# One woven stream against two passes: attention and token mixing of all pairs first, channel mixing afterwards

## The chip, the cores and the metric

One core of one Trainium2 chip. The metric is the device time of one execution in microseconds (us), the median of several executions. Everything is computed in fp32. On TensorE one fp32 matmul instruction leaves two records in the trace, and "records" below means those.

## The reference, cut to what matters

```python
# q, k, v: (8 batches, 8 heads, 576 tokens, 64 channels)
kv  = np.einsum('bhsd,bhse->bhde', k, v)
out = np.einsum('bhsd,bhde->bhse', q, kv)
rms = np.sqrt(np.mean(out * out, axis=-1, keepdims=True) + 1e-06)
x   = out / rms * g_norm                 # then to (batch, token, 512)

xt = x.transpose(0, 2, 1)                # token mixing, 576 -> 256 -> 576
u  = x + (np.maximum(xt @ w_tok1, 0.0) @ w_tok2).transpose(0, 2, 1)
h2 = np.maximum(u @ w_ch1, 0.0) @ w_ch2  # channel mixing, 512 -> 1536 -> 512
return u + h2
```

The four mixing weights arrive as float64. The kernel rounds them to fp32 on the chip with seven elementwise steps per piece ("decode"), each weight once. A batch has 576 = 4 x 128 + 64 tokens. Two batches make a pair, whose two leftovers of 64 tokens share one tile, so a pair has nine tiles and there are four pairs.

## The kernel before

Attention and token mixing of a pair ("the front") are woven, step by step, into the channel mixing of the pair before. The first front has nothing to be woven into. The decode of the token weights and of the first 12 pieces of channel weights is woven into it, and that of the other 12 into the first layer of channel mixing.

```python
def decode(dst, raw):                    # cut: names of operands kept
    nc.gpsimd.tensor_scalar(out=dst, in0=hi, ...)                 # 1 GpSimd
    nc.vector.tensor_scalar(out=dst, in0=dst, ... min, max)       # 2 VectorE
    nc.vector.tensor_scalar(out=bits, in0=bits, ... shift)        # 3 VectorE
    nc.vector.scalar_tensor_tensor(out=bits, in0=hi, in1=bits)    # 4 VectorE
    nc.vector.tensor_scalar(out=part, in0=bits, ... mask)         # 5 VectorE
    nc.vector.scalar_tensor_tensor(out=part, in0=lo, in1=part)    # 6 VectorE
    nc.gpsimd.tensor_tensor(out=dst, in0=dst, in1=part, op=ALU.add)  # 7 GpSimd

def kv(side, half):                      # k^T v, two heads' pairs at once
    for i in range(2):
        for j in range(JJ):              # the fifth piece has 64 rows only
            r = slice(0, P if j < J else HF)
            nc.tensor.matmul(ps[:, i], lhsT=k_in[r, j, ts(i, P)],
                             rhs=v_in[r, j, ts(i, P)], ...)

def norm(o_ps, i):                       # one tile of 128 tokens
    nc.scalar.activation(x3, o, AF.Square)
    nc.vector.tensor_reduce(ms, x3, ...)
    ...                                  # root and a Newton step, small
    nc.vector.tensor_mul(x3, o, inv.to_broadcast([P, H, D]))
    nc.gpsimd.tensor_mul(x3, x3, g_sb.to_broadcast([P, H, D]))

weave(steps, weights)                    # first front with 17 pieces of weights
for pair in range(B // 2):
    body = main(pair, X, U)              # channel mixing
    if pair == 0:
        weave(body[:NF], [do(get_ch2, f) for f in range(NF)])
        body = body[NF:]
    if pair + 1 < B // 2:
        X, U, fill = front(pair + 1)
    weave(body, fill)
```

## Time and profile before

| | before |
|---|---|
| time, median of 4 runs | 1053.81 us |
| span of the profiled execution | 1052.2 us |
| TensorE busy | 1002.1 us, 95% |
| VectorE, ScalarE, GpSimd busy | 25%, 10%, 10% |
| first token layer of the first pair | 60.4 to 80.9 us |
| channel weights decoded until | about 168 us |
| dense period of a pair | 244.96 us |

One view is added here: the chain of work that ended last, where channel mixing waits for the last piece of its weights. The columns are start, duration, engine, tile and line.

```profile
162.63 1.49 DVE w_ch L114
...
164.60 0.70 DVE w_ch L118
...
166.63 1.27 POOL w_ch L124
167.90 0.04 issue
167.94 2.08 PE ps_w L287 x2
```

The seven steps of a decode run one after the other on two engines, and TensorE starts the second layer of channel mixing (ps_w) 0.04 us after the last of them.

### The profile page before, as it was taken

What the parts mean: (1) busy time and instruction counts of PE and PEld (TensorE: products, weight loads), DVE (VectorE), ACT (ScalarE), POOL (GpSimd) and SP (SyncE); (2) the same over time, 40 slices, a digit from 0 to 9 for tenths busy, and PEclk for the clock granted to TensorE, in tenths of its full rate; (3) what the DMA queues carried; (4) which work ended last, traced back from release to release, by engine and by line L of the source; (5) the groups of instructions that cost most, each with busy time, mean ns of one, the idle gap of its engine ahead of it and who ended that gap; (6) DMA issues with size and microseconds to landing.
All of it is one profiled execution on the core that took longest, in us unless ns stands there. A gap on an engine that the chain in (4) does not pass through costs nothing.

```text
span 1052.2 us, 7658 instructions
## 1 busy us (share of the span) xinstructions
PE 1002.1 (95%) x3120; PEld 537.9 (51%) x3120; DVE 266.5 (25%) x559; ACT 100.8 (10%) x214; POOL 106.1 (10%) x100
## 2 busy tenths in 40 slices
PE   4788977999999999999999999999999999999998
PEld 3643544664455466554445456554445445454553
DVE  2898773351011113330111112240011111010000
ACT  0211100020001011111001011011001000000000
POOL 1464441120000001110000000010000000000000
PEclk9789997999999999999999999999999999999999
DMA  8943342121000031300000021000000000000000
GB/s 239 323 147 116 108 142 95 66 90 55 10 11 1 20 100 46 111 10 1 10 21 1 10 65 45 11 20 1 0 21 11 10 21 0 21 10 11 21 0 30
DMA packets 33554, 53.34 MB, mean 51 GB/s; under 512 B 2416, under 2 KB 20848, under 8 KB 33520
## 3 DMA queue, kind: packets, MB, share of 16 engines
q1 hardware_dynamic: 28928, 37.76, 11.0%
q10 hardware_dynamic: 4592, 15.11, 4.6%
q8 instruction: 24, 0.39, 0.2%
q14 instruction: 10, 0.08, 0.0%
HBM read 43.42 MB, written 9.44 MB: 50 GB/s over the span
## 4 chain that ended last, share of the span: by engine, by line
PE 84%; DVE 9%; DMA 4%; POOL 2%; issue 1%; ACTq 0%; ACT 0%; POOLq 0%
PE ps_w L287 35%; PE ps_v L273 33%; PE ps_h L224 4%; PE ps_u L235 4%; PE ps_kv L171 3%; PE ps_o L206 2%; DMA raw<-in_moe_w_tok_dram 2%; DVE part L122 2%; DVE w_ch L118 1%; DVE w_ch L116 1%; DVE w_ch L114 1%; PE ps_h L227 1%; PE ps_ut L250 1%; DVE part L120 1%; POOL w_ch L124 1%; DMA raw<-in_moe_w_ch_dram 1%
## 5 line engine op out<-in xcount | busy, mean ns | idle before, releaser
L287 PE MATMUL ps_w<-w_ch,v 128*128 128x512 f32 x864 | 385.0, 598 | 10.5 <-POOL w_ch L124 10.5
L273 PE MATMUL ps_v<-uT,w_ch 128*128 128x384 f32 x1152 | 383.8, 488 | 1.1 <-DVE v L279 1.1
L273 PEld LDWEIGHTS ps_v<-uT,w_ch 128*128 128x128 f32 x1152 | 215.0, 190 | 151.7 <-issue 13.4
L287 PEld LDWEIGHTS ps_w<-w_ch,v 128*128 128x128 f32 x864 | 161.7, 191 | 208.8 <-issue 190.9
L279 DVE TENSOR_SCALAR v<-ps_v 128x384 f32<-128x384 f32 x72 | 40.0, 556 | 266.2 <-PE ps_v L273 266.2
L201 POOL TENSOR_TENSOR x<-x,g_sb 128x512 f32<-128x512 f32 x36 | 47.8, 1328 | 519.5 <-DVE x L200 517.7
L291 DVE TENSOR_TENSOR o<-ps_w,x 128x512 f32<-128x512 f32 x36 | 24.9, 692 | 259.0 <-PE ps_w L287 258.9
L171 PE MATMUL ps_kv<-v_in,k_in 128*128 128x128 f32 (+1 forms) x320 | 56.0, 323 | 14.9 <-DMA v_in<-in_v_dram 13.8
L277 ACT ACTIVATE v<-ps_v 128x384 f32<-128x384 f32 x72 | 35.3, 490 | 355.2 <-PE ps_v L273 326.4
L235 PE MATMUL ps_u<-h,w_tok 128*128 128x512 f32 x128 | 60.3, 596 | 3.4 <-DVE x L243 3.3
L171 PEld LDWEIGHTS ps_kv<-v_in,k_in 128*128 128x128 f32 (+1 forms) x320 | 48.6, 219 | 27.1 <-issue 20.8
L224 PE MATMUL ps_h<-x,w_tok 128*128 128x512 f32 x128 | 59.7, 610 | 1.7 <-DVE ms L188 1.7
L243 DVE TENSOR_TENSOR x<-ps_u,x 128x512 f32<-128x512 f32 x36 | 24.8, 689 | 96.1 <-PE ps_u L235 78.3
L206 PEld LDWEIGHTS ps_o<-kvp,qT 128*128 128x128 f32 x256 | 37.1, 214 | 16.6 <-issue 4.4
L206 PE MATMUL ps_o<-kvp,qT 128*128 128x128 f32 x256 | 38.6, 302 | 7.1 <-DVE x L200 3.7
L251 ACT COPY uT<-ps_ut 128x512 f32<-128x512 f32 x36 | 21.0, 585 | 219.3 <-PE ps_ut L250 199.8
L187 DVE TENSOR_REDUCE ms<-x 128x8 f32<-128x512 f32 x36 | 24.5, 683 | 67.5 <-ACT x L185 67.5
L224 PEld LDWEIGHTS ps_h<-x,w_tok 128*128 128x128 f32 x128 | 24.7, 195 | 32.1 <-issue 28.9
L235 PEld LDWEIGHTS ps_u<-h,w_tok 128*128 128x128 f32 x128 | 23.8, 190 | 29.8 <-issue 21.1
L124 POOL TENSOR_TENSOR w_ch<-w_ch,part 128x512 f32<-128x512 f32 x24 | 31.4, 1308 | 36.7 <-DVE part L122 34.8
L185 ACT ACTIVATE x<-ps_o 128x512 f32<-128x512 f32 x36 | 21.5, 597 | 90.1 <-PE ps_o L206 75.3
L250 PEld LDWEIGHTS ps_ut<-ident,x 128*128 128x128 f32 x144 | 17.7, 141 | 20.8 <-issue 16.9
(38 smaller groups left out, 281.1 us busy)
## 6 DMA issues: line engine op xcount, KB each, us to landing
raw<-in_moe_w_ch_dram ACTq DMA_DIRECT2D x24, 512.0 KB, 3.6
qT<-in_q_dram SPq DMA_DIRECT2D x8, 1152.0 KB, 5.6
k_in<-in_k_dram SPq DMA_DIRECT2D x16, 512.0 KB, 3.7
v_in<-in_v_dram SPq DMA_DIRECT2D x16, 512.0 KB, 5.5
out_dram<-o SPq DMA_DIRECT2D x32, 256.0 KB, 2.0
raw<-in_moe_w_tok_dram ACTq DMA_DIRECT2D x2, 576.0 KB, 6.1
raw<-in_moe_w_tok_dram ACTq DMA_DIRECT2D x2, 512.0 KB, 9.2
k_in<-in_k_dram SPq DMA_DIRECT2D x16, 64.0 KB, 3.6
```

The costliest lines, as they stand in the source:

```text
L124: nc.gpsimd.tensor_tensor(out=dst, in0=dst, in1=part, op=ALU.add)
L171: nc.tensor.matmul(ps[:, i], lhsT=k_in[r, j, ts(i, P)], rhs=v_in[r, j, ts(i, P)], start=(j == 0), stop=(j == JJ - 1))
L201: nc.gpsimd.tensor_mul(x3, x3, g_sb.to_broadcast([P, H, D]))
L206: nc.tensor.matmul(ps[:, ts(hp, P)], lhsT=qT[side][:, hp, ts(j, P)], rhs=kvp[side][:, hp], start=True, stop=True)
L224: nc.tensor.matmul(ps, lhsT=w_tok1[:, j, ts(t, P)], rhs=X[side * J + j], start=(j == 0), stop=False)
L235: nc.tensor.matmul(ps, lhsT=w_tok2[:, t, ts(i % J, P)], rhs=h1[i // J][:, t], start=(t == 0), stop=(t == NTOK - 1))
L250: nc.tensor.transpose(ps[:, c], X[i][:, ts(c, P)], ident)
L273: nc.tensor.matmul(ps, lhsT=w_ch1[:, c, ts(f, P)], rhs=U[blk][:, c], start=(c == 0), stop=(c == NC - 1))
L277: nc.scalar.activation(dst, ps, AF.Relu)
L279: nc.vector.tensor_scalar(out=dst, in0=ps, scalar1=0.0, scalar2=None, op0=ALU.max)
L287: nc.tensor.matmul(ps, lhsT=v1[i // TB, part][:, f, ts(i % TB, P)], rhs=w_ch2[:, ft], start=(ft == 0), stop=(ft == NF - 1))
L291: nc.vector.tensor_tensor(out=o, in0=ps, in1=X[i], op=ALU.add)
```

## The change

The intent is to have TensorE never wait for channel weights, and to use larger and simpler matmuls. There are two passes. The first does attention and token mixing of all four pairs and stores the result u in DRAM; the channel weights are fetched and decoded behind it. The second reads u back in nine groups of 512 tokens and does channel mixing alone. k and v get zero rows so that each matmul of k-v has 128 rows; normalisation takes two tiles at a time; the 64-row matmuls of the two batches in the first token layer stand next to each other; the first decode step goes to ScalarE and the second to GpSimd.

```diff
@@ decode
-        nc.gpsimd.tensor_scalar(out=dst, in0=hi.bitcast(F32), scalar1=2.0 ** -112, scalar2=1.0,
-                                op0=ALU.mult, op1=ALU.mult)
-        nc.vector.tensor_scalar(out=dst, in0=dst, scalar1=TOP, scalar2=-TOP,
+        nc.scalar.activation(dst, hi.bitcast(F32), AF.Copy, scale=2.0 ** -112)
+        nc.gpsimd.tensor_scalar(out=dst, in0=dst, scalar1=TOP, scalar2=-TOP,
                                 op0=ALU.min, op1=ALU.max)
@@ kv
-                    r = slice(0, P if j < J else HF)
-                    nc.tensor.matmul(ps[:, i], lhsT=k_in[r, j, ts(i, P)],
-                                     rhs=v_in[r, j, ts(i, P)],
+                    nc.tensor.matmul(ps[:, i], lhsT=kk[:, j, ts(i, P)], rhs=vv[:, j, ts(i, P)],
@@ norm: two tiles (n = 2)
-            nc.gpsimd.tensor_mul(x3, x3, g_sb.to_broadcast([P, H, D]))
+            nc.gpsimd.tensor_mul(x3, x3, g_sb.to_broadcast([P, n * H, D]))
@@ first token layer, both sides of a pair
+            for side in range(2):
+                r = ds(side * HF, HF)
+                nc.tensor.matmul(ps[side], lhsT=w_tok1[r, J, ts(t, P)], rhs=x_of(pair, 8)[r], ...)
@@ the order of the whole (cut)
-    weights += [do(get_ch1, i, c) for i in range(DCH // 512) for c in range(NC)]
-    weave(steps, weights)
-    for pair in range(B // 2):
-        ...
+    weave(attention(0), weights)                # token weights only
+    weights = [do(get_ch1, i, c) for i in range(2) for c in range(NC)]
+    weights += [do(get_ch2, f) for f in range(NF)]
+    steps = []
+    for pair in range(B // 2 - 1):
+        weave([do(steps.append, f) for f in token_mixing(pair)],
+              [do(steps.append, f) for f in attention(pair + 1)])
+    weave(steps, weights)
+    ...
+    weave(token_mixing(3), prepare(0, ...))     # prepare: transposes of a group
+    ...
+    for g in range(NG):
+        fetch_u(g + 1)
+        for f in range(NF):
+            channel1(g, f)
+        weave(channel2(g), prepare(g + 1, t_psum))
```

## The prediction

> **What bounds the kernel now.** I read the busy strips first, then one table of stretches, then the end of the chain of waits, then the timeline of single steps. The strips are in 40 slices of 26.3 us, in tenths:
>
> ```profile
> span 1052.2 us, 7658 instructions
> ...
> PE   4788977999999999999999999999999999999998
> ...
> DVE  2898773351011113330111112240011111010000
> ...
> PEclk9789997999999999999999999999999999999999
> ```
>
> TensorE is short of work only in the first seven slices, exactly where VectorE is at 7 to 9, and there its clock is below full in several slices. The stretches give it in numbers (columns: us, then busy us of PE, PEld, DVE, ACT, POOL, then clock, DMA share, GB/s):
>
> ```profile
> 33.36:166.63 133.27, 107.35 (x350) 59.05 (x348) 109.67 (x206) 18.49 (x40) 63.50 (x60) 0.88 0.49 155
> ...
> 372.22:617.18 244.96, 244.96 (x782) 131.21 (x781) 43.91 (x104) 24.61 (x53) 11.40 (x9) 1.00 0.10 34
> 617.18:862.13 244.95, 244.95 (x781) 131.20 (x781) 43.89 (x104) 24.61 (x53) 11.40 (x9) 1.00 0.06 20
> 862.13:1052.20 190.07, 185.58 (x504) 95.41 (x503) 16.55 (x28) 9.41 (x19) 0.00 (x0) 1.00 0.04 14
> ```
>
> The middle two are the two undisturbed periods of a pair of batches: TensorE never idle, VectorE at 18%. The first runs from the first to the last decode of a channel weight: VectorE is 82% busy. The end of the chain of waits gives the parts of a period (start, us, what):
>
> ```profile
> 862.13 30.96 PE ps_v L273 x96
> 893.09 30.90 PE ps_w L287 x72
> ...
> 1016.81 30.91 PE ps_w L287 x72
> ...
> 1047.75 0.69 DVE o L291
> ```
>
> A block of channel mixing is 61.86 us, three are 185.58, so attention and token mixing of a pair ("the front") cost 244.96 - 185.58 = 59.38. Four dense pairs would be 979.8. The tail is 1052.2 - 1047.75 = 4.5. So 1052.2 - 979.8 - 4.5 = 67.9 us are lost at the start. Where in the start? Token mixing of the first pair begins at 60.4 in the timeline. By then only attention is done. From the same steps seen dense later, the front's 59.38 holds 18.4 us of first token layer (4 x (3.53 + 1.06)), 15.6 of second (8 x 1.72 + 1.87) and 4 of transposes (9 x 0.44), with which attention and the joints between steps come to about 20.6. So 40 us are lost by 60.4, and the other 28 later, when channel mixing waits for its weights.
>
> Single steps, dense:
>
> ```profile
> 377.22 2.97 PE L171 MATMUL ps_kv<-v_in,k_in 128*128 128x128 f32 x20
> ...
> 380.13 2.20 PE L273 MATMUL ps_v<-uT,w_ch 128*128 128x384 f32 x6
> ...
> 393.56 1.05 PE L206 MATMUL ps_o<-kvp,qT 128*128 128x128 f32 x8
> ...
> 394.45 1.78 PE L273 MATMUL ps_v<-uT,w_ch 128*128 128x384 f32 x5
> ...
> 471.23 1.12 PE L227 MATMUL ps_h<-x,w_tok 64*128 64x512 f32 x2
> ...
> 472.29 2.85 PE L273 MATMUL ps_v<-uT,w_ch 128*128 128x384 f32 x8
> ```
>
> Start to start (an fp32 matmul is two records): 20 records of k-v take 2.91 us, though 8 of the same width in attention take 0.89, or 0.111 each. Four of the twenty have only 64 rows. Two 64-row records of token mixing take 1.06, against 30.90/72 = 0.429 each for full ones of that width, 0.86.
>
> **What the Trainium skill says.** "TensorEngine Tiling (Array Packing)", Key Properties: a change of tiling mode drains TensorE. The trace agrees: 16 full records at 0.111 leave 2.91 - 1.78 = 1.13 us for four 64-row ones, 0.28 each. "TensorE: Matmul & The Clock Gate", The mechanism (Part 3): matmuls on different row groups run concurrently. This kernel never has two such neighbours; its two column halves in the left-over tile of the second token layer do overlap (8 records in 103.97 to 105.84, 1.87 us instead of 3.43). "SBUF — State Buffer", Who interferes with whom: GpSimd excludes a VectorE instruction with two SBUF inputs, or in a 2-port mode, for a whole instruction. It agrees:
>
> ```profile
> 95.34 0.41 DVE L116 TENSOR_SCALAR w_ch<-w_ch 128x512 uint32<-128x512 uint32 x1
> ...
> 98.58 1.38 POOL L124 TENSOR_TENSOR w_ch<-w_ch,part 128x512 f32<-128x512 f32 x1 [1.56 <-DVE part L122]
> 98.86 1.37 DVE L116 TENSOR_SCALAR w_ch<-w_ch 128x512 uint32<-128x512 uint32 x1
> ```
>
> The same shift takes 0.41 us alone and 1.37 beside GpSimd's add.
>
> **The change part by part.**
> TensorE work. Zero rows make every k-v matmul 128 rows: 20 x 0.111 = 2.22 instead of 2.91, 0.69 saved x 16 steps = 11 us. The two sides' 64-row matmuls of the first token layer become neighbours: twice 1.06 per pair of sides; if the second record of one side overlaps the first of the other, 3 x 0.43 + 0.2 = 1.5, saving 0.6 x 8 = 5; I take 6 for both this and fewer mode changes. Channel mixing has the same columns: 384 cost 30.96/96 = 0.3225 and 512 cost 0.429, so a column is as dear, and 288 records fewer save (0.3225 x 4/3 - 0.429) x 864 = 0.7 us. Total 979.8 - 17.7 = 962.
>
> Second pass. Tokens are transposed from a single buffer, four per group, the last one right before the first layer of the next group. Transposes to dependent matmul: 526.82 to the copy's start at 527.45 is 0.63, the copy 0.58, and say 0.07 to the matmul: 1.28, against 0.44 when other work follows (371.62 to 372.06). So 0.84 x 8 groups = 7 us of bubbles that before does not have. The tail stays 4.5. One hand-over between passes and one exposed ReLU in the last token mixing: 1 us.
>
> DRAM round trip. 9.44 MB written and read again. Reads are 1 MB, asked for one group (82 us) ahead; hidden. In the first pass 28.3 MB of q, k, v, 15.1 of weights and 9.4 stored, 53 MB in some 230 us, is 230 GB/s, against 323 in the second slice at a share of 0.98. Hidden on the mean.
>
> Start. Only the five token-weight pieces are woven into the first attention; the 24 channel-weight pieces (now 20, some larger) come after it. Before, the last k-v of the pair started at 38.17, set by transfers that mostly remain, but attention then took until 58.8 because VectorE was decoding channel weights (TensorE waited 3.7 us on the normalisation). Now: k-v until 41, three attention steps of 4 to 5 us until 46, a normalisation of two tiles about 8 until 54, overlapped with first-layer work and next-pair k-v of about 6. Attention now costs 20.6 - 2.8 = 17.8, so 54 - 17.8 - 6 = 30; I take 29 lost, instead of 40. The later 28 us of weight waits vanish as such.
>
> First pass, steady. Three stretches of token mixing plus the next attention: (59.38 - 4 - 4.3) x 3 = 153 us of TensorE. VectorE in it, by undisturbed durations: decode now has 4 instead of 5 operations here (0.43 + 0.69 + 0.43 + 0.69 = 2.24) x 24 = 54; normalisation of two tiles 1.22 + 1.22 + 0.8 (an estimate: 512 elements take 0.69, of which 0.53 is 512 elements at the 0.96 GHz that "Trainium Kernel Development and Optimization", NeuronCore Architecture, gives for VectorE; twice 0.53 and once the other 0.16; 0.8 for the five small steps of 0.11 to 0.2) 3.24 x 4 + 2.2 per pair, x 3 = 45; adds 27 x 0.69 = 19; copies 12 x 0.28 = 3. Sum 121. In the first stretch above the mean of a decode shift is 739 ns where its median is 428, of the step before it 604 against 426, of the mask 524 against 427: with the small steps that wait up to 1.36 us beside GpSimd, about 18 us of the 110 are such waiting, a fifth on top of the rest. With a fifth, 121 is 145. VectorE reached 82% there, held up by the chain GpSimd, VectorE, GpSimd of each piece and its two staging buffers. The weights are now thinner on the ground (20 pieces in 153 us, 7.7 us each, where that chain took 9.1 us for two), so I choose 86%: 145 / 0.86 = 168. So VectorE, not TensorE, bounds this stage by a little: 15 us more.
>
> Sum: 962 + 29 + 15 + 7 + 4.5 + 1 = 1018.
>
> **Rivals.** One: VectorE work hides completely. For it: the weights have 153 us instead of 133, VectorE gives up one operation per piece and half of its tiny normalisation steps. Against it: 145 of 153. Then 1003. Two: a new wait takes the old one's place. The first decode step moves from GpSimd to ScalarE, which also issues the weight transfers, so ScalarE can stand waiting for a transfer (3.6 us median to landing) with squares, ReLUs and k-v copies behind it. For it: before, ScalarE's uT copy already waited 12.4 us behind weight staging. Against: ScalarE is nearly idle, and TensorE has four-deep PSUM. At 2 us exposed for each of 20 pieces, 1055. Three: GpSimd, whose work on two tiles doubles the lock to about 2.5 us, stretches VectorE further: 10 to 20 more, 1030 to 1038. Four: transfers, if bursts of q, k, v, weights and stores collide: 10 more.
>
> **Range and chances.** The floor is rival one with a start better by 5: 998. Above, rival three plus some of two: 1040. Faster by 2% needs less than 1032.6 of 1053.7, which leaves 15 us for errors; I give that 0.78, within 2% 0.19, slower 0.03 (rival two at its full size).
>
> **What would show it.** Second pass: nine groups of 82.4 us, about 0.8 us idle before each first matmul, full clock, VectorE under 15%. k-v steps near 2.2 us. Token mixing starting near 46 to 54. First-pass stretch of 160 to 175 us from there to the last pair's token mixing, VectorE above 80%, TensorE short of work there. The prediction is wrong if TensorE is at 95% or more there (rival one), if ScalarE's longest waits are on the raw weight transfers (rival two), or if the second pass shows bubbles of several us.

## The result, and the profile after

The changed kernel takes 1054.62 us (median of 4 runs, 1053.17 to 1056.12) against 1053.81. The ratio is 1.0015, with a 95% interval of 0.9997 to 1.0033: the same time. A ratio here is the mean time of one kernel's fast runs over that of the other's in the same rounds, so it is not quite the ratio of the medians quoted. The predicted 1018 was missed by 37 us.

The page of the changed kernel, in the same 40 slices:

```profile
span 1052.0 us, 6896 instructions
...
PE   3759787899999999999999999999999999999998
...
DVE  2886877635210010001001001000000100100000
...
PEclk9879988999999999999999999999999999999999
```

The hole in TensorE's strip is as wide as before, seven to eight slices, and VectorE is again busy in just those. From slice 9 on little is left to gain. Next the three stretches of the first pass, each from the end of one pair's first token layer to that of the next (columns as in the prediction: the stretch, its length, busy us of PE, PEld, DVE, ACT, POOL, clock, DMA share, GB/s):

```profile
83.45:149.70 66.25, 55.67 (x242) 32.17 (x240) 52.29 (x85) 15.90 (x28) 31.53 (x24) 0.92 0.65 218
149.70:215.75 66.05, 56.30 (x243) 32.87 (x241) 41.87 (x72) 12.35 (x23) 21.74 (x16) 0.92 0.56 179
215.75:268.50 52.75, 51.10 (x242) 30.04 (x240) 23.27 (x48) 9.08 (x18) 10.67 (x5) 1.00 0.44 150
83.45:268.50 185.05, 163.07 (x722) 95.08 (x720) 117.44 (x204) 37.33 (x69) 63.94 (x45) 0.94 0.56 184
```

All three hold the same matmuls. The third, after the last decode, takes 52.75 us; the first two take 13.3 us more each. In neither is any engine full: over all three VectorE is at 117 of 185 us, or 63%, and TensorE at 88%. The granted clock is 0.92 in the first two, and the same 242 records keep TensorE busy some 5 us longer there than in the third; the other 8 to 9 us are idle.

What TensorE waits for in the first pass (waiter, releaser, us in total, times, longest):

```profile
PE ps_h L247 <- POOL x L212: 20.4, 8, 7.9
PE ps_o L219 <- ACT kvp L188: 13.8, 4, 6.2
PE ps_kv L184 <- DMA v_in<-in_v_dram: 13.1, 2, 12.8
PE ps_o L228 <- ACT kvp L188: 7.1, 2, 5.2
```

Before, 10.5 us of waits stood against the decode's last add (GpSimd, w_ch). That releaser is gone; in its place the first token layer (ps_h) waits 20.4 us for the last step of the normalisation, and attention (ps_o) 20.9 us for the copies of k-v on ScalarE. Both are steps that share engines with the decode.

The longest of these waits, step by step, in the order of the timeline (start, duration, engine, line, operation, tiles; an idle time in brackets):

```profile
55.28 1.41 DVE L130 SCALAR_TENSOR_TENSOR w_ch<-raw,w_ch 128x768 uint32<-128x768 uint32 x1
...
58.58 0.55 DVE L132 TENSOR_SCALAR part<-w_ch 128x768 uint32<-128x768 uint32 x1
...
60.35 3.08 POOL L212 TENSOR_TENSOR x<-x,g_sb 128x1024 f32<-128x1024 f32 x1 [4.46 <-DVE x L211]
61.16 2.31 DVE L206 SCALAR_TENSOR_TENSOR ms<-ms,inv 128x16 f32<-128x16 f32 x1
...
63.40 2.60 POOL L136 TENSOR_TENSOR w_ch<-w_ch,part 128x768 f32<-128x768 f32 x1
...
63.49 1.22 PE L247 MATMUL ps_h<-x,w_tok 128*128 128x512 f32 x1 [7.86 <-POOL x L212]
```

TensorE waits for the double tile that GpSimd multiplies at 60.35; it has stood idle for 7.86 us when that ends. Steps of channel-weight decode (here lines 130 and 132, 1.41 and 0.55 us) run on VectorE between the small steps of this tile's normalisation. While the multiply runs, a VectorE step on 16 elements per partition, which belongs to another tile, takes 2.31 us and ends when the multiply does. Two decodes of channel weights are in progress beside it (line 136 is the last step of one), although in the program the channel weights come after this attention. Their first transfer is issued at 32.3 us and their first decode step runs at 37.4 us: the order in the program text isn't the order on the engines.

The second pass, from the chain that ended last:

```profile
371.41 0.02 issue
371.43 0.59 ACT uT L293
372.02 0.04 issue
372.07 41.47 PE ps_v L311 x96
413.53 20.60 PE ps_w L325 x48
```

TensorE stands still from 371.41 to 372.07, 0.66 us between two groups, while ScalarE copies the last transposed tile. It does so eight times, 5.3 us in all by this chain; the run below that moves the transposes won back 760.4 - 755.9 = 4.5 us of it. The last matmul ends at 1047.35 us, as good as before (1047.75). The pass starts at 286.97 us, so it takes 760.4 us.

The steps of attention, dense (the numbers after the operation count records):

```profile
207.43 1.12 PE L251 MATMUL ps_h<-x,w_tok 64*128 64x512 f32 x2
...
214.69 1.13 PE L251 MATMUL ps_h<-x,w_tok 64*128 64x512 f32 x4
215.75 2.50 PE L184 MATMUL ps_kv<-v_in,k_in 128*128 128x128 f32 x20
218.08 1.88 PE L260 MATMUL ps_u<-h,w_tok 128*128 128x512 f32 x4
219.80 2.39 PE L184 MATMUL ps_kv<-v_in,k_in 128*128 128x128 f32 x20
222.03 1.88 PE L260 MATMUL ps_u<-h,w_tok 128*128 128x512 f32 x4
```

From start to start a k-v step takes 222.03 - 219.80 = 2.23 us, against 2.91 before. The 64-row matmuls are neighbours only in the second half of the layer, where four records take 215.75 - 214.69 = 1.06 us, the time of two. In the first half they stay apart.

In a table, with the prediction's parts. Its text gives 4.5 us for the tail and, for the second pass, nine groups of 82.4, eight times 1.76 of transposes and eight bubbles of 0.84, together 762. So its first pass ended at 1018 - 4.5 - 762 = 251.5; less 18.4 after the last first layer (15.6 of second layer, 1.8 of transposes, 1 of hand-over) and the 168 of the three stretches, its start is 65.

| us | predicted | after | run without channel weights |
|---|---|---|---|
| end of the first pair's first token layer | 65 | 83.5 | 72.0 |
| three stretches | 168 | 185.1 | 158.3 |
| from there to the second pass | 18.4 | 18.5 | 18.4 |
| start of the second pass | 251.5 | 287.0 | 248.75 |
| second pass to its last matmul | 762 | 760.4 | 760.4 |

The last column is an experiment told below. The whole miss lies ahead of the second pass.

### The profile page after: what moved, and what is told of

It reads as the page before. It is cut to its first block, busy times and chain, and to the rows that moved or that the text cites. A ratio compares the mean times of both kernels' runs of the same rounds, so it can differ in the third digit from the quotient of the medians.

```text
span 1052.0 us, 6896 instructions
## 1 busy us (share of the span) xinstructions
PE 986.1 (94%) x2832; PEld 475.5 (45%) x2832; DVE 238.3 (23%) x384; ACT 109.4 (10%) x189; POOL 101.8 (10%) x80
## 4 chain that ended last, share of the span: by engine, by line
PE 78%; DVE 1%; ACT 1%; issue 0%; POOLq 0%
PE ps_v L311 35%; PE ps_w L325 35%; PE ps_u L260 3%; PE ps_h L247 2%; PE ps_ut L292 1%; PE ps_kv L184 1%; PE ps_o L219 1%; ACT uT L293 1%; PE ps_h L251 0%; POOLq L418 0%; DVE ms L198 0%; PE ps_u L265 0%; DVE ms L199 0%; DVE x L211 0%; ACT x L196 0%
## 5 line engine op out<-in xcount | busy, mean ns | idle before, releaser
L311 PE MATMUL ps_v<-uT,w_ch 128*128 128x512 f32 x864 | 373.2, 593 | 3.0 <-ACT uT L293 3.0
L311 PEld LDWEIGHTS ps_v<-uT,w_ch 128*128 128x128 f32 x864 | 163.4, 190 | 207.5 <-issue 202.3
L317 DVE TENSOR_SCALAR v<-ps_v 128x512 f32<-128x512 f32 x54 | 37.3, 691 | 346.0 <-PE ps_v L311 346.0
L327 DVE TENSOR_TENSOR xg<-ps_w,xg 128x512 f32<-128x512 f32 x36 | 24.9, 691 | 353.4 <-PE ps_w L325 353.4
L247 PE MATMUL ps_h<-x,w_tok 128*128 128x512 f32 x128 | 66.7, 665 | 20.4 <-POOL x L212 20.4
L315 ACT ACTIVATE v<-ps_v 128x512 f32<-128x512 f32 x54 | 32.2, 597 | 316.7 <-PE ps_v L311 316.7
L184 PE MATMUL ps_kv<-v_in,k_in 128*128 128x128 f32 x320 | 40.9, 285 | 13.1 <-DMA v_in<-in_v_dram 13.1
L212 POOL TENSOR_TENSOR x<-x,g_sb 128x1024 f32<-128x1024 f32 (+1 forms) x20 | 44.1, 2207 | 69.3 <-DVE x L211 55.1
L184 PEld LDWEIGHTS ps_kv<-v_in,k_in 128*128 128x128 f32 x320 | 40.0, 201 | 20.2 <-issue 18.7
L136 POOL TENSOR_TENSOR w_ch<-w_ch,part 128x512 f32<-128x512 f32 (+1 forms) x20 | 31.9, 1597 | 32.1 <-DVE part L134 32.1
L260 PEld LDWEIGHTS ps_u<-h,w_tok 128*128 128x128 f32 x128 | 23.7, 201 | 21.6 <-issue 20.4
L292 PEld LDWEIGHTS ps_ut<-ident,xg 128*128 128x128 f32 x144 | 17.5, 141 | 15.6 <-issue 15.3
L198 DVE TENSOR_REDUCE ms<-x 128x16 f32<-128x1024 f32 (+1 forms) x20 | 22.1, 1104 | 7.6 <-ACT x L196 7.6
L134 DVE SCALAR_TENSOR_TENSOR part<-raw,part 128x512 f32<-128x512 uint32 (+3 forms) x25 | 22.8, 911 | 0.3
```

Of the source, the lines that this page charges most:

```text
L184: nc.tensor.matmul(ps[:, i], lhsT=kk[:, j, ts(i, P)], rhs=vv[:, j, ts(i, P)], start=(j == 0), stop=(j == JJ - 1))
L212: nc.gpsimd.tensor_mul(x3, x3, g_sb.to_broadcast([P, n * H, D]))
L247: nc.tensor.matmul(ps[side], lhsT=w_tok1[:, j, ts(t, P)], rhs=x_of(pair, side * J + j), start=(j == 0), stop=False)
L260: nc.tensor.matmul(ps, lhsT=w_tok2[:, t, ts(i % J, P)], rhs=h1[i // J][:, t], start=(t == 0), stop=(t == NTOK - 1))
L292: nc.tensor.transpose(ps[:, c], xg[g][:, i, ts(c, P)], ident)
L311: nc.tensor.matmul(ps, lhsT=w_ch1[:, c, ts(f, P)], rhs=uT[g][:, c], start=(c == 0), stop=(c == NC - 1))
```

## The experiments

All of them measure against the kernel before in the same rounds, with three rounds each. Where the text gives the start, the stretches or the start of the second pass, it is from the one profiled execution, which can be a few us off the median: for the runs with late weights alone and with the first early transposes it is the fastest of the four, 3 and 4 us below the median, and for the run without the multiply by g the slowest, 3 us above. Their expectations use letters for three theories. W: the loss is the work of decoding the channel weights beside the attention. D: it is not, and lies in what stays when the decode is gone, which is the order of work, the transfers and the chain of the normalisation. S: it is ScalarE, which has got the first decode step and also issues the transfers of the weights. "Stretches" are those of the table above; after the change they are 66.3, 66.0 and 52.8 us, behind a start of 83.5 us. "Late weights" means the second layer's weights.

### Decode taken out, in both kernels

The channel weights are still transferred, but only one step of the decode remains (wrong result).

```diff
# in the changed kernel; in the kernel before the same with the one step on GpSimd
-        decode(w_ch1[:, c, ts(i, FH)], raw)
+        nc.scalar.activation(w_ch1[:, c, ts(i, FH)], raw[..., 1].bitcast(F32), AF.Copy, scale=2.0 ** -6)
# and for w_ch2 likewise
```

> The changed kernel with the channel weights' decode cut to its first operation (wrong result on purpose; the transfers stay). Theory W (the decode work on VectorE and GpSimd stretches the first pass, which ends at 287 us instead of some 250): the pair-to-pair periods of 66 us fall to 52 to 54 and the first pass ends near 245 to 255, total 1010 to 1022. Rival D (the transfers of weights, q, k, v and stores are what is short): the first pass still ends after 275, total above 1040.

> The kernel before with the same cut. If the 28 us that it loses after 60.4 us are decode work, 1020 to 1030; if they are transfers, 1045 or more. Together with the run above: if the first pass of the changed kernel gains more than this one, the change made the decode dearer in time.

Measured: 1030.63 us for the changed kernel (ratio 0.9775, 0.9755 to 0.9796) and 1032.68 for the kernel before (0.9798, 0.9777 to 0.9820). The decode costs the changed kernel 287.0 - 264.9 = 22.1 us of its first pass, and the kernel before some 20 (1032.68 is just above the range expected for decode work). So neither theory holds as it stood: W gets 22 us of the 37 missed, D the rest. It also means that the change did not take the decode off the path. It costs as much in its new place as in the old.

### Zero-padding alone

```diff
 # kernel before, with fixed k and v buffers whose last 64 rows are set to zero once
-                    nc.tensor.matmul(ps[:, i], lhsT=k_in[r, j, ts(i, P)], rhs=v_in[r, j, ts(i, P)],
+                    nc.tensor.matmul(ps[:, i], lhsT=k_in[:, j, ts(i, P)], rhs=v_in[:, j, ts(i, P)],
```

> One part of the change alone: the kernel before with zero-padded k and v. The step of k-v falls from 2.91 to 2.25 us; 16 of them are 10.5 us. If the gain of TensorE work counts (12 of the 16 steps lie in dense stretches), 1043 to 1046; if it is given back at the start, 1050 or more.

Measured: 1046.58 us, correct, ratio 0.9939 (0.9921 to 0.9958). The span of its profiled execution is 7.5 us shorter, against 12 dense k-v steps at 0.69 = 8.3 (the four of the first pair lie in the starved start). This is a small miss of the expected range, but the size per step holds: the twelve later steps take 2.23 us each, as in the changed kernel. What reaches the total is 6 to 7.5 us, not the 11 that the prediction counts for all sixteen.

### The decode's old engines

```diff
-        nc.scalar.activation(dst, hi.bitcast(F32), AF.Copy, scale=2.0 ** -112)
-        nc.gpsimd.tensor_scalar(out=dst, in0=dst, scalar1=TOP, scalar2=-TOP,
+        nc.gpsimd.tensor_scalar(out=dst, in0=hi.bitcast(F32), scalar1=2.0 ** -112, scalar2=1.0,
+                                op0=ALU.mult, op1=ALU.mult)
+        nc.vector.tensor_scalar(out=dst, in0=dst, scalar1=TOP, scalar2=-TOP,
```

> One part of the change undone: the decode's first step on GpSimd and the second on VectorE, as before. Theory S (ScalarE stands waiting for weight transfers, with k-v copies and squares behind it, and TensorE waits for those): 10 to 30 us faster, 1025 to 1045. Theory W: VectorE gets one operation more per piece (24 x 0.43 = 10 us and more beside GpSimd), so 0 to 15 us slower, 1054 to 1070.

Measured: 1054.93 us, correct, ratio 1.0011 (0.9989 to 1.0033). The start gets 10 us later (93.5) and the two stretches with decode 4 and 3 us shorter. Nothing is gained, so a cost of the size that S names isn't seen. The edit can't exclude a smaller one, because it also gives VectorE one step more per piece. A later run puts a size on it.

### No channel weights at all

No transfers and no decode of channel weights; they are set to a constant (wrong result).

```diff
     def get_ch1(i, c):
-        raw = fetch(FH)
-        ...
+        pass
     def get_ch2(f):
-        ...
+        pass
+    for t in (w_ch1, w_ch2):
+        nc.vector.memset(t, 0.02)
```

> The changed kernel with neither transfers nor decode of the channel weights (a constant in their place, wrong result on purpose). The cut decode alone gave 22 us: the first token layer of the first pair ended at 77.5 us instead of 83.5, the first stretch took 63.4 instead of 66.3, the second 52.8 instead of 66.0. Theory T (what is left of the late start is the channel weights' transfers, which compete with q, k and v and make ScalarE wait): that layer ends at 62 to 68 and all stretches take 52 to 54, total 1005 to 1013. Rival N (the start is q, k, v and a long normalisation chain of their own): it ends at 74 to 78, total 1017 to 1026.

Measured: 1015.84 us (1015.52 to 1015.95), ratio 0.9629 (0.9615 to 0.9643). Its first two stretches, columns as above:

```profile
72.00:124.70 52.70, 51.08 (x242) 30.04 (x240) 23.30 (x48) 9.09 (x18) 10.68 (x5) 1.00 0.55 180
124.70:177.50 52.80, 51.15 (x242) 30.05 (x240) 23.28 (x48) 9.08 (x18) 10.68 (x5) 1.00 0.55 180
```

A stretch is now as short as the third one after the change, and TensorE is busy 97% of it at the full clock. The channel weights cost the first pass 287.0 - 248.75 = 38.2 us. The predicted 1018 is about what the changed kernel takes when it has no channel weights to load. That is chance: the 15 us that the prediction did add for VectorE stand against 12.3 us that it lacked elsewhere. The expectation was met in part: the stretches are those of theory T, the start lies between its range and the rival's. A start of 72.0 against 65 shows that the prediction was also 7 us short in what weights have no part in. (The constant is set by two VectorE steps of 5.18 us; they end at 14.76 us, and VectorE then idles for 2.5 us, so they hold nothing up.)

The whole first pass with the weights and without, columns as above:

```profile
0.00:286.97 286.97, 228.10 (x976) 134.25 (x977) 176.08 (x294) 58.41 (x103) 101.85 (x80) 0.92 0.60 195
0.00:248.75 248.75, 216.80 (x976) 129.61 (x977) 118.83 (x216) 44.44 (x83) 54.01 (x40) 0.97 0.54 174
```

The same 976 records keep TensorE busy 11.3 us longer with the weights, at a lower granted clock. So of the 38.2 us TensorE is idle for 26.9, and the rest is slower matmuls. No run changes the clock by itself, so why it is lower there stays open.

### Where between 22 and 38

The one step that e1 leaves in place is moved from ScalarE to GpSimd. The transfers stay.

```diff
-        nc.scalar.activation(dst, hi.bitcast(F32), AF.Copy, scale=2.0 ** -6)
+        nc.gpsimd.tensor_scalar(out=dst, in0=hi.bitcast(F32), scalar1=2.0 ** -6, scalar2=1.0,
+                                op0=ALU.mult, op1=ALU.mult)
```

> As the run of the changed kernel without decode, but the one operation that is left of it lies on GpSimd instead of ScalarE (wrong result on purpose; all transfers stay). Against no weights at all, that run still lost 16 us of the first pass: 5.5 before the end of the first token layer, 10.7 in the first stretch. Theory S (ScalarE waits for the weight transfers in its own queue and holds up k-v copies, squares and roots): the 16 us vanish, first token layer near 72, first stretch near 53, total 1013 to 1018. Theory D (the transfers take the bandwidth from q, k and v): nothing changes, 1027 to 1033.

Measured: 1027.44 us (ratio 0.9747, 0.9733 to 0.9762); the second pass starts at 260.4 instead of 264.9. So about 4.5 us come from ScalarE standing behind transfers with work in its queue. That is close to the noise: the medians differ by 3.2 us, and the intervals of the two ratios overlap. Of the theories, S expected 16 us here and D none. Then 260.4 - 248.75 = 11.6 us remain that only the transfers (and one short step per piece) can make. Its first 54 us:

```profile
0.00:54.00 54.00, 26.28 (x152) 20.91 (x152) 27.57 (x53) 11.35 (x19) 19.28 (x26) 0.91 1.00 303
```

The DMA engines are at a share of 1.00, where the run without channel weights has 0.79 in the same 54 us: q, k, v and the channel weights want the same time. The 38.2 us thus divide into 22.1 of decode, 4.5 of ScalarE's waiting and 11.6 of transfers. The order of removal matters for such a division: with less decode the transfers also come faster. The three add up to 38.2 because they were taken away one after another, and each holds idle time and slower matmuls together.

### Weights held back until the first attention is done

The channel weights get their own staging buffers, whose memory is free only when the last normalised double tile of the first pair is done.

```diff
     weave(attention(0), weights)
+    gate = ExitStack()
+    g_tile = pool("gate", 1, "left", gate).tile([P, 4608], F32, name="g_tile")
+    nc.gpsimd.tensor_copy(g_tile[:, :1], X[0, 3][:, 0, :1])
+    gate.close()
+    stages.append(pool("stage_ch", 2, "left", left))
```

> All work kept, but the channel weights' staging buffers are given memory that comes free only with the last normalised tile of the first pair, so that no channel weight is fetched or decoded before. Theory T: the first token layer of the first pair ends at 64 to 70 instead of 83.5; the decode then falls on three stretches instead of two and a bit; total 1036 to 1046. Rival (the decode costs the same wherever it lies): what the start gains the stretches lose, 1050 to 1058.

Measured: 1053.48 us, correct, ratio 0.9985 (0.9969 to 1.0002). The start ends at 74.1 instead of 83.5, but the first two stretches take 74.4 and 68.0 instead of 66.3 and 66.0, and the second pass starts at 288.1. The 9.4 us gained are given back in the two stretches, as the rival expected. Moving the weights inside the first pass is not enough, as what they cost moves with them.

### Second-layer weights later

The 12 pieces of second-layer weights are fetched and decoded in the last token mixing and beside the first layer of the first group, where VectorE has little to do.

```diff
-    weights += [do(get_ch2, f) for f in range(NF)]
+    later = [do(get_ch2, f) for f in range(NF)]
@@ last token mixing
+    weave(steps, later[:5])
@@ second pass
-        for f in range(NF):
-            channel1(g, f)
+        weave([do(channel1, g, f) for f in range(NF)], later[5:] if g == 0 else [])
```

> The 12 pieces of the second channel weights (half of the elements) are fetched and decoded during the last token mixing and the first group's first layer, where VectorE was 21% and 8% busy. If decode beside token mixing is what stretches 52.8 us to 66, the stretches give back about half of 27 us and the total is 1036 to 1043; if the second layer of the first group then waits for its weights, 1050 or more.

Measured: 1037.07 us, correct, ratio 0.9835 (0.9817 to 0.9853). The total is in the expected range. The first three stretches, columns as above:

```profile
84.00:138.55 54.55, 51.78 (x243) 30.31 (x241) 33.19 (x60) 11.59 (x21) 18.59 (x11) 1.00 0.57 191
138.55:191.30 52.75, 51.09 (x242) 30.04 (x240) 23.30 (x48) 9.08 (x18) 10.67 (x5) 1.00 0.58 180
191.30:246.67 55.37, 51.15 (x243) 30.05 (x241) 32.01 (x59) 11.69 (x22) 15.37 (x11) 1.00 0.54 181
```

The first two fall by 25.0 us together, and the clock is 1.00 in both. The late pieces were decoded from 232 to 290 us, six of them before the second pass starts at 267.0 and six beside its first layer. The first six lengthen the third stretch by 2.6 us and what follows it by 1.9; the second pass still takes 760.4 us. So the same 12 pieces, transfers and decode together, cost 25 us beside attention, 4.5 beside the last token mixing and nothing that shows beside channel mixing. The net gain is 20.0 us in this execution and 17.6 by the medians. This is the clearest confirmation of the cause, by a kernel with a correct result.

### Normalisation one tile at a time

```diff
-            ps = ps_o.tile([P, 2, DM], F32, name="ps_o", tag="o")
             for t in range(2):
+                ps = ps_o.tile([P, 1, DM], F32, name="ps_o", tag="o")
                 ...
-            norm(ps, c, 2)
+                norm(ps, x[:, t:t + 1])
# four accumulators of one bank instead of two of two banks
```

> The normalisation undone to one tile of 128 tokens at a time, four accumulators of one bank instead of two of two banks. Theory L (the 2.35 us multiplication on GpSimd locks VectorE out twice as long, and two accumulators make attention wait): 5 to 12 us faster. Rival (VectorE's work is what counts, and 80 more small operations cost 0.15 to 0.25 us each): 5 to 15 us slower.

Measured: 1044.12 us, correct, ratio 0.9896 (0.9869 to 0.9924). The start ends at 74.3, and the stretches (66.9, 66.9, 50.5) hardly change. The gain is of the expected size and lies in the start, where TensorE has little but this chain to wait for. The edit also makes four accumulators of two, so the run doesn't tell the shorter chain from the additional accumulators.

### Both, with the gate, and with earlier transposes

Late weights and single tiles together; the same with the gate; the same with the last transposes of the next group ahead of the last tile of this one:

```diff
-        weave(channel2(g), prepare(g + 1, t_psum))
+        tiles, turn = channel2(g), prepare(g + 1, t_psum)
+        for step in tiles[:1] + turn[:1] + tiles[1:2] + turn[1:2] + tiles[2:3] + turn[2:] + tiles[3:]:
+            step()
```

> The two gains put together: second channel weights late, normalisation one tile at a time. If they are separate (17 and 10 us), 1025 to 1029; if both only make room on the same engine, VectorE, 1031 to 1037.

> The same, and no channel weight before the first pair's tiles are normalised. With only 8 pieces left for the stretches, the gate that gave nothing with 20 should help by up to the 9 us that the start gained there: 1016 to 1024. If those 8 pieces cost as much in the first stretch, 1025 to 1031.

> Late second weights and single tiles again, and in the second pass the last transposes of a group before its last tile instead of after it. Each of eight bubbles of 0.66 us before a first layer goes: 5 us less than without, 1019 to 1024. If TensorE's order is kept by something else, no change.

Measured: 1037.71 (ratio 0.9853), 1036.54 (0.9833) and 1032.57 us (0.9800, 0.9765 to 0.9834), all correct. Late weights gained 17.6 us and single tiles 10.5, but together they gain no more than the late weights alone (the expected range for shared room was 1031 to 1037). The natural reading is that both drew on the same idle time. The gate again moves time from the start (67.6 instead of 77.5) into the next stretch (69.6 instead of 61.0), and misses both ranges of its expectation, 1016 to 1024 and 1025 to 1031. The earlier transposes give some 5 us by the medians and 4 in the second pass, as expected; the expected total, 1019 to 1024, was missed because it built on a gain that the two runs before it didn't show.

### Which way GpSimd's multiply costs

Still open was how decode and attention cost each other so much with VectorE below 80%. The prediction's third rival says that GpSimd's two-tile multiply shuts VectorE out. The alternative is that the first token layer waits at the end of a long chain, whatever its steps. The multiply by g was halved, and left out altogether (wrong result).

```diff
-            nc.gpsimd.tensor_mul(x3, x3, g_sb.to_broadcast([P, n * H, D]))
+            for t in range(n):
+                xt = x3[:, t * H:(t + 1) * H]
+                nc.gpsimd.tensor_mul(xt, xt, g_sb.to_broadcast([P, H, D]))
# second run: no multiply at all
```

> The changed kernel, GpSimd's multiply by g as two instructions of one tile each instead of one of two tiles; result correct. Lock theory (the third rival of the prediction: one GpSimd instruction of 2.4 us keeps VectorE out for that long, so that the length of the instruction is what costs): this alone gives most of what normalising one tile at a time gave (10.4 us), 1044 to 1048. Chain theory (what costs is that a token layer waits for the whole chain of a double tile, which stays as long): 1052 to 1056.

> The changed kernel without the multiply by g (wrong result on purpose), 44 us of GpSimd's work in the first pass gone. Lock theory: 15 to 20 us less, 1035 to 1040, since VectorE is then shut out only by the decode's own GpSimd steps. Chain theory: each chain in front of a token layer becomes 2.4 us shorter, about four such waits in the start and the two stretches with decode, 8 to 10 us less, 1044 to 1047. If GpSimd's multiply costs nothing on the path: 1053 to 1056.

Measured: 1046.43 us in halves (correct, ratio 0.9933, 0.9918 to 0.9948) and 1031.42 without (ratio 0.9789, 0.9773 to 0.9805). The first agrees with the lock theory's number, but not with its place. Its start is the same (84.5) and so is the first stretch (66.5); the gain is in the second, 57.0 instead of 66.0, where the decode is over earlier (its last add starts at 178.2 us instead of 184.4). The second gains more than either theory said, and its stretches show where:

```profile
71.40:138.00 66.60, 58.36 (x242) 32.73 (x240) 52.84 (x88) 16.06 (x27) 24.55 (x19) 0.90 0.70 233
...
198.70:249.30 50.60, 50.60 (x242) 30.21 (x240) 22.20 (x48) 9.10 (x18) 0.00 (x0) 1.00 0.47 156
```

The start is 12.1 us earlier, the second stretch 5 shorter (60.7) and the third 2.2 shorter, with TensorE at 50.60 of 50.60 us. Only these last 2.2 us lie in a stretch with no decode, so they are what the chain costs by itself. The first stretch is no shorter: the chain of waits has a transfer of channel weights of 8.35 us in it, and many short steps of decode and normalisation in turn. So the multiply costs where a decode runs beside it. How much of that is the lock and how much its own time in the chain isn't settled by these runs, because leaving it out takes both away.

The best version was then tried without the single tiles, and with the multiply in halves:

> The changed kernel with the second layer's weights fetched and decoded late (1037 measured) and the last transposes of a group ahead of its last tile (5 us of bubbles), the normalisation still two tiles at a time; result correct. If the gains of late weights and of single-tile normalisation come from the same slack, this is as fast as with both: 1031 to 1034. If single-tile normalisation still gave its part: 1034 to 1038.

> As the run before it, with the multiply by g in halves; result correct. Lock theory: 4 to 6 us less than that run, in the start and in the one stretch that still has a decode beside it. Chain theory: within 2 us of that run.

Measured: 1031.65 us (correct, ratio 0.9797, 0.9780 to 0.9815) and 1034.05 us (correct, 0.9816, 0.9801 to 0.9830). The first is as fast as with single tiles, so these can be left out: the slack was the same. The halves gain nothing here, where the lock theory expected 4 to 6 us. They helped with 20 decodes beside the attention and not with 8. The chain of the first of these kernels at a handover between two groups:

```profile
343.31 10.30 PE ps_w L325 x24
353.61 6.44 PE ps_v L311 x15
```

The first layer of the next group now follows the last tile with no gap. This kernel, late weights and early transposes on top of the change, is about 2% faster than the kernel before; its interval, 0.9780 to 0.9815, reaches across the 2% line, so by that measure the verdict is unclear.

## Why the prediction was wrong

What held, term by term:

- k-v steps: predicted 2.22 us, measured 2.23. The mixed-height matmuls did cost what the trace of the kernel before let one work out.
- The second pass: predicted 762 us, measured 760.4, with bubbles of 0.66 us instead of 0.84. The round trip through DRAM is hidden: TensorE is idle only in the bubbles, at the full clock.
- The 64-row matmuls: 6 us predicted. Before, eight records per pair took 4 x 1.06 = 4.24 us. After, two groups of two at 1.05 and one of four at 1.06 take 3.16, so 4 x 1.08 = 4.3 us were gained. Half of the neighbours in the program text were scheduled apart.
- A stretch without decode: the prediction had 153 / 3 = 51 us of TensorE; the trace has 51.1 busy.

What failed is the pair of steps "Start" and "First pass, steady". The prediction wrote that "the later 28 us of weight waits vanish as such" and that the stretches take "145 / 0.86 = 168. So VectorE, not TensorE, bounds this stage by a little: 15 us more". It treated the channel weights as VectorE work that starts after the first attention, and let the one engine's busy time set the stage. The runs show something else: VectorE had 117 us of work in the three stretches, less than the 145 (some of the decode had been done before them), in 185 us of time: a share of 63%, where the prediction named one above 80% as a sign of its being right. No engine was full. The channel weights cost 38.2 us of the first pass, not 15. Taken away one after another, the decode was worth 22.1, ScalarE's queue standing behind transfers 4.5, and the transfers 11.6. That the decode costs by its steps between those of a normalisation for which TensorE waits is read from the traces, as in the wait above; the amounts are from the runs. The weights also began at 32 us, inside the first attention, so the waits didn't vanish: they moved there.

The rest of the miss, 248.75 - (251.5 - 15) = 12.3 us, has nothing to do with channel weights: the start was 7 us too optimistic, and the three stretches take 158.3 us instead of 153 even without weights, because each has a wait of some 1.6 us before its first token layer (52.7 less 51.1). With 38.2 - 15 = 23.2 these make the 35.5 us by which the second pass started late. A slip in the prediction's sums plays no part: 59.38 less 18.4, 15.6 and 4 is 21.4, not 20.6, which moves the loss at the start by less than 1 us.

The rivals were the right ones, but they were weighed as alternatives, and their sizes were guessed with mixed success. Rival one (all hides, 1003) falls. Rival two, ScalarE behind its transfers, is real: ScalarE waited 27.5 us for raw weights in 11 waits. But TensorE saw about 4.5 us of it, not 40, and moving the step to GpSimd, with another to VectorE, gained nothing. Rival three, GpSimd's longer instruction, is worth 8 us in the run with halves, against 10 to 20. Rival four was put at 10 and measured at 11.6. None of them alone is the miss. How far rival three's 8 us lie within the decode's 22.1 was not tested, so they can't simply be added.

On the lock, the Trainium skill, "SBUF — State Buffer", Who interferes with whom, says that a VectorE instruction with two SBUF inputs contends with a GpSimd instruction that reads SBUF. This trace agrees: a step of 16 elements with two SBUF inputs took 2.31 us at 61.16, ending with GpSimd's multiply. But it is not the whole cause, as the run without the multiply shows by its first stretch, which stays at 66.6 us.

So where did the expected gain go? The dense work did shrink. Before it is 979.8 us. After, the second pass has 9 x 82.4 + 8 x 1.76 = 755.7 us, and the first pass, at the 50.6 us per pair that the run without the multiply shows to be possible, 4 x 50.6 + 1.8 = 204 us; that is 20 us less. Lost time grew by as much: before 67.9 us were lost at the start, after 287.0 - 204 = 83 us in the first pass and some 5 in bubbles. Of the 83, TensorE is idle for 287.0 - 228.1 = 58.9; in the rest the same matmuls take longer. The weights that channel mixing had waited for are now in the way of attention, and the first pass has only 204 us of TensorE work to hide them, where the second has 760 with VectorE at 8%.

## What to carry to other kernels

Moving a load to where an engine is less than full doesn't hide it: look at whose dependent chain it will sit in, and put it where TensorE works for long from data that are already there. The same 12 pieces of weights cost 25 us beside attention and 4.5 us where they were put instead. When several mechanisms each have a plausible cost, ask what they come to together before taking the chances. And test first with the whole suspect removed (here all channel weights): that one run gave the size of what all the others had to explain.

## What the Trainium skill lacked or had wrong

- "TensorEngine Tiling (Array Packing)", Key Properties, names the drain at a change of tiling mode but gives no size. Here a 64-row record among 128-row ones costs 0.28 us instead of 0.111, and a k-v step of 20 records went from 2.91 to 2.23 us by padding to full height.
- "TensorE: Matmul & The Clock Gate", The mechanism (Part 3), holds for row groups in fp32: four 64-row records on two row groups took 1.06 us, where two alone take 1.05. It doesn't say that the neighbours have to survive scheduling; half of them here didn't.
- "SBUF — State Buffer", Who interferes with whom, is right about the lock, but it gives no figure for what it costs small instructions: a VectorE step on 16 elements took 2.31 us beside a multiply of 1024. In the changed kernel, cutting that multiply in two gained 8 us (1054.6 to 1046.4), and with fewer decodes beside it nothing (1031.7 to 1034.1).
